# The sign step of a float64 to float32 conversion as a one-operand step on 16-bit halves, in a recurrent attention and MLP kernel

## The chip, the cores and the metric

One Trainium2 (trn2) chip; the program runs on one core. The metric is the device time of one execution in microseconds (us), as the median of several runs. Engines are named as in the profile: PE (TensorE), PEld (its weight loads), DVE (VectorE), ACT (ScalarE), POOL (GpSimd) and SP (SyncE, which issues most DMAs).

## The reference

```python
# attention: B=4, H=8, S=768, D=48, float32
state = zeros(B, H, D, D)
for t in range(S):
    cur = u * outer(k_t, v_t)
    y_t = r_t @ (state + cur)
    state = w * state + outer(k_t, v_t)
# then, with x = y as [4, 768, 384]:
h = x^T @ U @ V                  # U [768, 32], V [32, 768], over the sequence
u = x + h^T
ch = relu(u @ w_ch1) @ w_ch2     # w_ch1 [384, 1536], w_ch2 [1536, 384]
return (u + ch).astype(float32)
```

The four matrices U, V, w_ch1 and w_ch2 come in float64 (normal draws, scaled, that nothing casts down). The other inputs are float32.

## The kernel before, in words

The attention is computed in chunks of 128 positions, six for each of the four batch rows; each chunk has score matmuls (`pab`, L751), state updates (`pab`, L766) and outputs (`pav`, L787 and L793), with small DVE steps between them (`am` L885, `S` L913, `rT` L721, `x` L892). Then comes the MLP: for each half of a batch row (384 positions), twelve hidden blocks of 128 columns go through `m_1` (nine matmuls `p<-uTh,w1s` and `p<-uTl,w1s`) and `m_2` (nine matmuls `p<-w2s,hh` and `p<-w2s,hl`). Every operand is split into a high part, rounded to the matmul's format, and a low part, the rest; ACT makes the high parts (`uTh` L1012, `hh` L1080, `w1s` and `w2s` L548), DVE or POOL the low ones (`uTl` L1013, `hl` L1081, `w1s`/`w2s` L549). The MLP of one batch row runs while the attention of the next one is slipped in between its matmuls; the first row's attention has nothing beside it but the loads and the weights.

The weights are loaded as 64-bit words and made float32 on the chip, 27 units in all: `raw_u`, two `raw_v`, and 24 `raw_w` of 128x384 (twelve for w_ch1, twelve for w_ch2). `unit(...)` defines four steps for each, on the tile seen as pairs of 32-bit words, `word(0)` the lower and `word(1)` the upper:

- the byte step: the top byte of the lower word, scaled to 0..7, written over the lower word. These become the last three bits of the float32 mantissa. ACT (L522) or DVE (L518), by a choice of the planner.
- the scale step: the upper word, read as float32 and multiplied by 2^-112, which moves the exponent into place. ACT (L534).
- the sign step, `sign()`: the upper word's top bit is taken and joined to the lower word. DVE (L525).
- the join step, `join()`: the upper word shifted left by 3, joined to the lower word. DVE (L528).

Then the split follows: the cast on ACT (L548) and the difference on DVE or POOL (L549). All of this is done once, and most of it falls into the first MLP of the first batch row.

The order on each engine is written by the program itself. `Plan` holds every operation with a cost in ns and a key (its due place), simulates the engines, and emits the instructions in the order of its simulated starts; for an operation with several possible engines it picks one. Costs are formulas: `dve(n)` is 130 + 1.09 n for n elements per partition, `act(n)` is 285 + 0.6 n, a one-operand step on DVE is put at 100 + 0.65 n. `lock=True` marks operations that the planner keeps from running beside POOL's. The planner also puts in `wake` matmuls, whose result is not used, where it sees PE waiting before the MLP starts: once it waits longer than 150 ns. Each engine runs its own list in order, so what stands behind a waiting instruction waits too.

Of the kernel before, what the change touches and what calls it, by code (L numbers as in the profile page):

```python
# [14 lines left out]
U16 = mybir.dt.uint16  # L15
AF = mybir.ActivationFunctionType
ALU = mybir.AluOpType
# [29 lines left out]
class Plan:  # L47
# [28 lines left out]
    def op(self, eng, ns, fn, w=(), r=(), alt=(), lock=False, dma=0.0, rows=0, late=0.0, tiled=False, dk=0.0):  # L76


        if self.direct:
            fn()  # L80
            return None
        o = Op()
        o.n = len(self.ops)
        o.key = (self.key + dk, o.n)
        o.ways = [(eng, ns, fn, lock)] + list(alt)
        o.dma, o.rows, o.late, o.tiled = dma, rows, late, tiled
        o.deps, o.behind, o.allocs, o.bufs = set(), set(), [], []
        for acc, write in [(a, False) for a in r] + [(a, True) for a in w]:
            b, sub = acc if isinstance(acc, tuple) else (acc, None)
            if not b.uses and b.tag:  # L90
                o.allocs.append(b)
                ring = self.rings.setdefault(b.tag, {"order": [], "next": 0, "free": [(0.0, "")] * b.bufs, "last": None})
                ring["order"].append(b)
            elif b.tag and b.uses[0][0] is not o:
                o.behind.add(b.uses[0][0])
            for p, s, pw in b.uses:
                if (write or pw) and (s is None or sub is None or s == sub) and p is not o:
                    o.deps.add(p)
            b.uses.append((o, sub, write))
            if b not in o.bufs:  # L100
                o.bufs.append(b)
                b.left += 1
        self.ops.append(o)
        return o
# [171 lines left out]
def dve(n):  # L276
    return 130 + 1.09 * n


def act(n):  # L280
    return 285 + 0.6 * n
# [7 lines left out]
def rwkv_moe(ctx: ExitStack, tc: tile.TileContext, r, k, v, w, u, U, V, w1, w2, out):  # L289
    nc = tc.nc  # L290
# [30 lines left out]
    op = plan.op  # L321
# [30 lines left out]
    def on_act(n, fn, w_, r_, times=1, dk=0.0):  # L352
        return op("ACT", times * (act(n) - 94) + 94, fn, w_, r_, dk=dk)
# [10 lines left out]
    def dma(fn, w_, r_, rows, run, eng="SP", ns=470, dk=0.0, late=0.0, either=False):  # L364

        q = nc.scalar if eng == "ACT" else nc.sync
        return op(eng, ns, lambda: fn(q), w_, r_, dma=rows * max(1.08 if run < 500 else 0.96, run / 400),
                  rows=rows, late=late, dk=dk, alt=[("ACT", ns, lambda: fn(nc.scalar), False)] if either else ())
# [113 lines left out]
    def big(shape, dt, name):  # L482
        return xbuf(shape, dt, "big", NBIG, name)
# [3 lines left out]
    def unit(name, shape, parts, split):  # L487

        P_ = shape[0]
        n = 1  # L490
        for s_ in shape[1:]:
            n *= s_
        raw = big([128, 2 * n], I32, f"raw_{name}") if wide else big([128, n], F32, f"raw_{name}")

        def view(ap):
            return ap if len(shape) == 2 else ap.rearrange("p (a c) -> p a c", a=shape[1])

        loaded = [(raw, i) for i in range(len(parts))]

        def load():  # L500
            for i, (p0, ap) in enumerate(parts):
                dma(lambda q, p0=p0, ap=ap: q.dma_start(view(raw.t[p0:p0 + ap.shape[0]]), ap.bitcast(I32) if wide else ap),
                    [(raw, i)], [], ap.shape[0], (8 if wide else 4) * n, ns=370, late=LATE)

        def word(i):
            return raw.t[:P_].rearrange("p (n two) -> p two n", two=2)[:, i]

        def byte():
            return raw.t[:P_].bitcast(U8).rearrange("p (n e) -> p n e", e=8)[:, :, 3]

        def fl():
            return view(word(0).bitcast(F32) if wide else raw.t[:P_])

        def on_dve_byte():
            nc.vector.tensor_scalar(word(0), byte(), 2.0 ** -5, 7.0, ALU.mult, ALU.min)  # L518

        def on_act_byte():  # L520

            nc.scalar.activation(word(0), byte(), AF.Copy, scale=7.49 / 255)  # L522

        def sign():
            nc.vector.scalar_tensor_tensor(word(0), word(1), -2 ** 31, word(0), ALU.bitwise_and, ALU.bitwise_or)  # L525

        def join():
            nc.vector.scalar_tensor_tensor(word(0), word(1), 3, word(0), ALU.logical_shift_left, ALU.bitwise_or)  # L528

        def convert():  # L530
            if wide:
                op("DVE", 100 + 0.65 * n, on_dve_byte, [(raw, "lo")], loaded, lock=True,
                   alt=[("ACT", act(n) + 100, on_act_byte, False)])
                on_act(n, lambda: nc.scalar.activation(word(1).bitcast(F32), word(1).bitcast(F32), AF.Copy,  # L534
                                                       scale=2.0 ** -112), [(raw, "hi")], loaded)
                op("DVE", dve(n), sign, [(raw, "lo")], [(raw, "hi")], lock=True)
                op("DVE", dve(n), join, [(raw, "lo")], [(raw, "hi")], lock=True)
            split(fl, raw)
        return load, convert

    def weight_units():
# [14 lines left out]
        def v_split(j, sl):  # L556
# [4 lines left out]
            return go  # L561

        units.append(unit("u", [128, NCH, R], [(0, U.rearrange("(c p) r -> p c r", p=128))], u_split))
        for j in range(S // DM):
            sl = slice(j * DM, (j + 1) * DM)
            units.append(unit(f"v_{j}", [3 * R, DM], [(i * R, V[:, sl]) for i in range(3)], v_split(j, sl)))
        for g in range(FG):
            for ct in range(NCT):
                units.append(unit(f"w1_{ct}_{g}", [128, DM],
                                  [(0, w1[ct * 128:(ct + 1) * 128, g * DM:(g + 1) * DM])],  # L570
                                  split_to(W1, (ct, g), f"w1s_{ct}_{g}")))
            for f in range(g * NFT // FG, (g + 1) * NFT // FG):
                units.append(unit(f"w2_{f}", [128, DM], [(0, w2[f * 128:(f + 1) * 128, :])],
                                  split_to(W2, f, f"w2s_{f}")))
# [770 lines left out]
```

## Time and profile before

| | |
|---|---|
| time, median of 3 runs | 438.04 us (437.14 to 439.49) |
| the profiled execution | 439.95 us, of which the span from first to last instruction is 437.9 us |
| mean granted PE clock | 0.984 |
| busy | PE 96%, PEld 91%, DVE 61%, ACT 33%, POOL 13% |

The profile is of one execution, and its own time (439.95 us) is 1.91 us above the median. A matmul's row in the trace is longer than the distance to the next one, since matmuls overlap; what tells of lost time on PE is the idle time ahead of a group of matmuls and what released it. The span falls into the first attention with the weights' loads (0 to 56.2 us), the first MLP pieces with the rest of the conversion (56.2 to about 100 us), and matmuls back to back from there to 429 us.

### The profile page before, as it was taken

The page shows a single profiled execution, that of the slowest core. Times are in us where ns is not written, and L with a number is a line of the kernel's source. Part 1 is how long each engine was busy: PE and PEld are TensorE (multiplying, and loading weights), DVE is VectorE, ACT ScalarE, POOL GpSimd, SP SyncE. Part 2 cuts the span into 40 slices and gives each one's busy share as a digit, 9 for nine tenths or more (in the row PEclk, how much of TensorE's full clock was granted, in tenths as well). Part 3 has the DMA queues.
Part 4 walks back from the last instruction along what each step waited for, and adds up shares of the span by engine and source line. Part 5 has one row for each costly group of instructions (what it writes and reads, how often), then busy time and mean ns, then how long its engine had stood idle before and what let it go on. Part 6 is the DMA issues. An engine that isn't in the chain of part 4 may idle for free.

```text
span 437.9 us, 12193 instructions
## 1 busy us (share of the span) xinstructions
PE 419.4 (96%) x5125; PEld 399.8 (91%) x5125; DVE 267.8 (61%) x602; ACT 142.9 (33%) x399; POOL 55.6 (13%) x92
## 2 busy tenths in 40 slices
PE   8889999999999999999999999999999999999991
PEld 8678899889999999999999999999999999999991
DVE  6979699999887757767775456567522351122121
ACT  1679679934421213121112221222112131111110
POOL 2651151223110002011100001101100000000000
PEclk9989699999999999999999999999999999999998
DMA  9979999654466876744586653231100510001001
GB/s 145 162 162 340 335 199 222 103 84 83 81 88 139 148 146 117 136 87 76 105 168 102 96 147 56 48 64 30 55 2 1 98 65 1 0 0 55 1 0 61
DMA packets 178975, 43.93 MB, mean 100 GB/s; under 512 B 168993, under 2 KB 175650, under 8 KB 178914
## 3 DMA queue, kind: packets, MB, share of 16 engines
q1 hardware_dynamic: 174162, 42.20, 46.9%
q10 hardware_dynamic: 4752, 0.89, 1.5%
q8 instruction: 42, 0.69, 0.7%
q14 instruction: 19, 0.16, 0.1%
HBM read 36.57 MB, written 6.49 MB: 98 GB/s over the span
## 4 chain that ended last, share of the span: by engine, by line
PE 81%; DVE 8%; ACT 3%; DMA 3%; POOL 1%; issue 1%; SPq 0%; ACTq 0%; DVEq 0%; POOLq 0%
PE p L344 64%; PE pav L787 5%; PE pav L793 4%; PE pu L344 3%; DVE raw_w L528 2%; DVE raw_w L525 2%; PE pab L751 2%; DMA ld<-in_r_dram 1%; DMA ld<-in_v_dram 1%; PE pab L766 1%; PE wake L344 1%; DVE hl L1081 1%; PE pG L958 1%; ACT dv L681 1%; POOL dv L671 1%
## 5 line engine op out<-in xcount | busy, mean ns | idle before, releaser
L344 PE MATMUL p<-uTh,w1s 128*128 128x384 f32 x576 | 148.2, 338 | 0.0
L1081 DVE SCALAR_TENSOR_TENSOR hl<-p,hh 128x384 fp32r<-128x384 f32 x96 | 53.2, 554 | 119.3 <-ACT hh L1080 119.0
L344 PE MATMUL p<-w2s,hh 128*128 128x384 f32 x576 | 120.3, 340 | 0.6 <-ACT hh L1080 0.6
L1080 ACT ACTIVATE hh<-p 128x384 fp32r<-128x384 f32 x96 | 47.2, 491 | 210.3 <-PE p L344 208.7
L344 PEld LDWEIGHTS p<-uTh,w1s 128*128 128x128 f32 x576 | 102.9, 188 | 0.8
L344 PEld LDWEIGHTS p<-w2s,hh 128*128 128x128 f32 x576 | 99.8, 188 | 2.8 <-ACT hh L1080 0.9
L344 PE MATMUL p<-uTl,w1s 128*128 128x384 f32 x288 | 96.4, 335 | 0.0
L344 PE MATMUL p<-w2s,hl 128*128 128x384 f32 x288 | 65.8, 335 | 0.0
L344 PEld LDWEIGHTS p<-uTl,w1s 128*128 128x128 f32 x288 | 54.0, 188 | 0.0
L344 PEld LDWEIGHTS p<-w2s,hl 128*128 128x128 f32 x288 | 51.4, 188 | 0.0
L787 PE MATMUL pav<-vsw,am 64*64 64x48 f32 x384 | 33.0, 226 | 0.6 <-DVE am L885 0.5
L793 PE MATMUL pav<-S,rT 48*64 48x48 f32 x704 | 32.0, 222 | 0.9 <-issue 0.9
L787 PEld LDWEIGHTS pav<-vsw,am 64*64 64x64 f32 x384 | 26.7, 137 | 6.1 <-issue 4.1
L751 PE MATMUL pab<-rT,kT 48*64 48x64 f32 x768 | 31.2, 228 | 0.3 <-DVE rT L721 0.2
L793 PEld LDWEIGHTS pav<-S,rT 48*64 48x64 f32 x704 | 27.9, 139 | 1.0 <-issue 1.0
L751 PEld LDWEIGHTS pab<-rT,kT 48*64 48x64 f32 x768 | 25.1, 137 | 1.5 <-DVE rT L721 0.5
L787 PE MATMUL pav<-ldv,am 64*64 64x48 f32 x320 | 26.5, 222 | 0.0
L787 PEld LDWEIGHTS pav<-ldv,am 64*64 64x64 f32 x320 | 21.5, 134 | 4.7 <-issue 3.9
L885 DVE TENSOR_TENSOR am<-pab,mask 128x256 f32<-128x256 f32 x48 | 19.7, 417 | 6.8 <-PE pav L793 6.2
L661 POOL MEMSET ks<- 128x128 f32 x24 | 4.9, 205 | 133.2 <-PE pab L766 66.8
L766 PE MATMUL pab<-ldv,ks 64*48 64x48 f32 (+1 forms) x576 | 21.0, 212 | 0.0
L926 ACT ACTIVATE SW<-S,wm 112x48 f32<-112x48 f32 x48 | 12.2, 324 | 21.3 <-DVE S L913 20.0
(127 smaller groups left out, 515.5 us busy)
## 6 DMA issues: line engine op xcount, KB each, us to landing
raw_w<-in_moe_w_ch_dram SPq DMA_DIRECT2D x24, 384.0 KB, 7.4
out_dram<-x SPq DMA_DIRECT2D x24, 192.0 KB, 2.0
ldr<-in_r_dram SPq DMA_DIRECT2D x20, 192.0 KB, 3.3
ldk<-in_k_dram SPq DMA_DIRECT2D x20, 192.0 KB, 3.6
ldv<-in_v_dram SPq DMA_DIRECT2D x20, 192.0 KB, 3.6
bl<-in_r_dram SPq DMA_DIRECT2D x79, 48.0 KB, 2.6
bl<-in_k_dram SPq DMA_DIRECT2D x79, 48.0 KB, 2.5
vsw<-in_v_dram SPq DMA_DIRECT2D x42, 48.0 KB, 3.2
```

The costliest lines, as they stand in the source:

```text
L344: return nc.tensor.matmul(*args, **kw)
L525: nc.vector.scalar_tensor_tensor(word(0), word(1), -2 ** 31, word(0), ALU.bitwise_and, ALU.bitwise_or)
L528: nc.vector.scalar_tensor_tensor(word(0), word(1), 3, word(0), ALU.logical_shift_left, ALU.bitwise_or)
L661: op("POOL", 250, lambda: nc.gpsimd.memset(ks.t[:, :, D:], 0.0), [(ks, "pad")], [])
L751: return [lambda q=q, i=i: nc.tensor.matmul(pt.t[(i ^ j) * C2:(i ^ j) * C2 + C2, q * C2:(q + 1) * C2], lhsT=kT.t[rows, q, i * C2:(i + 1) * ...
L766: return nc.tensor.matmul(pt.t[j * HP:j * HP + m, SU + q * D:SU + (q + 1) * D], lhsT=ks.t[half, 2 * q + j, :m], rhs=vt()[half, 2 * q + j, ...
L787: return nc.tensor.matmul(to(q, j, i), lhsT=am[j].t[half, q, :], rhs=vsw[n].t[half, q, :] if j else vt()[half, 2 * q, :], start=(row == RO ...
L793: return nc.tensor.matmul(to(q, row, i), lhsT=rT.t[rows, q, i * C2:(i + 1) * C2], rhs=St[n, i].t[rows, q, :], start=False, stop=(row == RO ...
L885: on_dve(256, lambda e: e.tensor_tensor(am.t, abs_[n][j].t[:, :SU].rearrange("p (h t) -> p h t", h=NP), mask_.unsqueeze(1).broadcast_to([1 ...
L926: nc.scalar.activation(dec.t[:, q], new.t[:, q], AF.Copy, scale=wm.t[:, q])
L1080: on_act(384, lambda: nc.scalar.activation(hh.t, pt.t[:, :TB], AF.Relu), [hh], [pt])
L1081: on_dve(384, lambda e: e.scalar_tensor_tensor(hl.t, pt.t[:, :TB], 0.0, f32(hh.t), ALU.max, ALU.subtract), [hl], [pt, hh])
```

## The change

The sign step no longer has two operands. The byte step now writes its 0..7 as a 16-bit number into the lowest quarter of the 64-bit word (`half(0)`), instead of a 32-bit number over the lower word. The sign step takes the uppermost quarter (`half(3)`), keeps its top bit, and writes the result as a 16-bit number into the next quarter (`half(1)`), where the byte step's input stood. The two halves are then the lower word as it was before, and the join step is as it was. The planner's cost of the sign step goes from 130 + 1.09 n to 100 + 0.65 n, for n = 384 from 549 to 350 ns. Nothing else is edited; in the changed kernel line numbers behind this place are 3 higher.

```diff
+        def half(i):
+            return raw.t[:P_].bitcast(U16).rearrange("p (n e) -> p n e", e=4)[:, :, i]
+
         def on_dve_byte():
-            nc.vector.tensor_scalar(word(0), byte(), 2.0 ** -5, 7.0, ALU.mult, ALU.min)
+            nc.vector.tensor_scalar(half(0), byte(), 2.0 ** -5, 7.0, ALU.mult, ALU.min)

         def on_act_byte():
-            nc.scalar.activation(word(0), byte(), AF.Copy, scale=7.49 / 255)
+            nc.scalar.activation(half(0), byte(), AF.Copy, scale=7.49 / 255)

         def sign():
-            nc.vector.scalar_tensor_tensor(word(0), word(1), -2 ** 31, word(0), ALU.bitwise_and, ALU.bitwise_or)
+            nc.vector.tensor_scalar(half(1), half(3), 0x8000, None, ALU.bitwise_and)
...
-                op("DVE", dve(n), sign, [(raw, "lo")], [(raw, "hi")], lock=True)
+                op("DVE", 100 + 0.65 * n, sign, [(raw, "lo")], [(raw, "hi")], lock=True)
```

Since the planner's costs set the order, instructions move. In the rows below, `raw_w_1_1` and `raw_w_2_1` are units of w_ch1's second group, `w1s_1` their split parts, `raw_w_2` and `raw_w_3` units of w_ch2; the last number of a name is a running number of the build.

DVE before, from the last of the six `uTl` that open the MLP on:

```order
L1013 TENSOR_TENSOR uTl_1_1095<-pu_1_2_970,uTh_1_1086 128x384
L549 TENSOR_TENSOR w1s_1_1102<-raw_w_0_1_749,w1s_1_1102 128x384
L1081 SCALAR_TENSOR_TENSOR hl_0_0_1127<-p_0_0_0_1082,hh_0_0_1116 128x384
L528 SCALAR_TENSOR_TENSOR raw_w_1_1_787<-raw_w_1_1_787 128x384
L1081 SCALAR_TENSOR_TENSOR hl_0_1_1149<-p_0_0_1_1104,hh_0_1_1141 128x384
L525 SCALAR_TENSOR_TENSOR raw_w_2_1_792<-raw_w_2_1_792 128x384
L525 SCALAR_TENSOR_TENSOR raw_w_2_735<-raw_w_2_735 128x384
L528 SCALAR_TENSOR_TENSOR raw_w_2_1_792<-raw_w_2_1_792 128x384
```

DVE now, from the steps of the same two units to the first `uTl` (sign is L528 and join L531 in the new numbers):

```order
L528 TENSOR_SCALAR raw_w_1_1_787<-raw_w_1_1_787 128x384
L528 TENSOR_SCALAR raw_w_2_1_792<-raw_w_2_1_792 128x384
L531 SCALAR_TENSOR_TENSOR raw_w_1_1_787<-raw_w_1_1_787 128x384
L531 SCALAR_TENSOR_TENSOR raw_w_2_1_792<-raw_w_2_1_792 128x384
L951 TENSOR_TENSOR Gs_1052<-wake,Gs_1052 32x384
L552 TENSOR_TENSOR w1s_1_1063<-raw_w_0_1_749,w1s_1_1063 128x384
L552 TENSOR_TENSOR w1s_1_1070<-raw_w_1_1_787,w1s_1_1070 128x384
L1016 TENSOR_TENSOR uTl_0_1090<-pu_0_0_856,uTh_0_1080 128x384
```

The sign and join of both units stood behind the first MLP block's low part (`hl`) and now stand ahead of `uTl`; on ACT the three casts `w1s_1` stand ahead of the six `uTh` as well, where before they stood behind them.

PE before, at the end of the first attention, where `wake<-x,Uf` gathers x^T U and `pu<-V` multiplies it by V:

```order
L344 MATMUL pu_1_1_1024<-ident,x_968 128x128
L344 MATMUL pu_1_2_970<-ident,x_968 128x128
L344 MATMUL wake<-x_1029,Uf 96x128 x3
L344 MATMUL wake_1041<-ident 128x128
L344 MATMUL pu_1_0_1021<-ident,x_1029 128x128
L344 MATMUL pu_1_1_1024<-ident,x_1029 128x128
L344 MATMUL pu_1_2_970<-ident,x_1029 128x128
L344 MATMUL wake_1041<-ident 128x128 x2
L344 MATMUL pu_0_0_855<-V_817,Gs_1047 128x384
```

PE now, at the same place:

```order
L344 MATMUL pu_1_1_1028<-ident,x_972 128x128
L344 MATMUL wake<-x_1030,Uf 96x128 x3
L344 MATMUL wake_1042<-ident 128x128
L344 MATMUL pu_1_2_970<-ident,x_972 128x128
L344 MATMUL pu_1_0_1026<-ident,x_1030 128x128
L344 MATMUL pu_1_1_1028<-ident,x_1030 128x128
L344 MATMUL pu_1_2_970<-ident,x_1030 128x128
L344 MATMUL wake_1042<-ident 128x128 x3
L344 MATMUL pu_0_0_856<-V_810,Gs_1052 128x384
```

One `pu` goes behind the last gathering matmuls, and one unused matmul is added; a second one is added behind the six `pu<-V`, just ahead of the MLP's first matmul. Earlier in that attention a few `pu` change place by one or two matmuls. PE then keeps its order up to the third block's second layer. Before, in the first MLP piece (`p_0_0_3` is the fourth block's first layer, `w2s_1188` with `hh_0_2` the third block's second layer):

```order
L344 MATMUL p_0_0_3_1204<-uTh_0_1067,w1s_1_1102 128x384 x2
L344 MATMUL p_0_0_3_1204<-uTl_0_1076,w1s_1_1102 128x384
L344 MATMUL p_0_0_1130<-w2s_1188,hh_0_2_1194 128x384 x2
L344 MATMUL p_1_0_1133<-w2s_1188,hh_0_2_1194 128x384 x2
L344 MATMUL p_2_0_1135<-w2s_1188,hh_0_2_1194 128x384 x2
L344 MATMUL p_0_0_3_1204<-uTh_0_1067,w1s_1_1151 128x384 x2
```

And now:

```order
L344 MATMUL p_0_0_3_1224<-uTh_0_1080,w1s_1_1063 128x384 x2
L344 MATMUL p_0_0_3_1224<-uTl_0_1090,w1s_1_1063 128x384
L344 MATMUL p_0_0_3_1224<-uTh_0_1080,w1s_1_1070 128x384 x2
L344 MATMUL p_0_0_3_1224<-uTl_0_1090,w1s_1_1070 128x384
L344 MATMUL p_0_0_3_1224<-uTh_0_1080,w1s_1_1073 128x384 x2
L344 MATMUL p_0_0_3_1224<-uTl_0_1090,w1s_1_1073 128x384
L344 MATMUL p_0_0_1146<-w2s_1169,hh_0_2_1203 128x384 x2
```

The whole fourth first layer now comes ahead of `hh_0_2`'s use. Further on, where the second batch row's attention begins, three groups of PE move ahead of MLP matmuls: a transpose `ptr` ahead of one pair `p<-w2s,hh`, the first scores `pab` ahead of one `m_1` part of three matmuls, and the first outputs `pav` ahead of two pairs `p<-w2s,hh`. From the pair behind those on, PE's order is the same in both kernels to the end. DVE also takes over one byte step from ACT (`raw_w_0_0`) and two `kT` scalings of that attention.

## The prediction

> **What bounds the kernel now.** I read the slices first, for the stages; then PE's busy time stage by stage; then PE's waits; then the chain, for what stands behind the waits.
>
> ```profile
> PE   8889999999999999999999999999999999999991
> DVE  6979699999887757767775456567522351122121
> ...
> PEclk9989699999999999999999999999999999999998
> ```
>
> ```profile
> 56.20:65.90 9.70, 9.13 (x54) 8.79 (x52) 9.54 (x18) 8.13 (x21) 4.40 (x5) 1.00 0.93 179
> 65.90:100.00 34.10, 32.61 (x342) 30.51 (x343) 33.92 (x71) 26.38 (x73) 8.24 (x10) 1.00 0.71 135
> 100.00:150.00 50.00, 50.00 (x819) 46.47 (x819) 42.12 (x99) 14.13 (x50) 5.52 (x10) 1.00 0.59 109
> ...
> 200.00:300.00 100.00, 100.00 (x1263) 95.66 (x1262) 64.37 (x148) 22.70 (x63) 9.33 (x16) 1.00 0.53 97
> 300.00:429.10 129.10, 129.02 (x1051) 126.48 (x1049) 40.93 (x83) 22.77 (x49) 2.54 (x3) 1.00 0.09 24
> ```
>
> In each stretch the columns are its length and the busy time of PE, PEld, DVE, ACT, POOL. From 56.2 to 100 us two engines are full: DVE 9.54 of 9.70 and 33.92 of 34.10, PE all but 0.57 and 1.49 us. From 100 us on PE has no idle time worth the name, and DVE has plenty. So whatever DVE gains, the end can move only by PE's idle time ahead of 100 us, and by the time at which the MLP starts (56.2 us). PE's waits from 56 us to the end are these five, and no others:
>
> ```profile
> PE p L344 <- ACT hh L1080: 0.6, 1, 0.6
> PE pav L787 <- DVE am L885: 0.5, 1, 0.5
> PE ptr L712 <- ACT kT L727: 0.4, 1, 0.4
> PE pab L751 <- DVE rT L721: 0.2, 1, 0.2
> PE ptr L712 <- DVE kT L733: 0.2, 1, 0.2
> ```
>
> Together 1.9 us. The chain of work that ended last says otherwise at first sight: it gives DVE 8%, with the two conversion steps on it.
>
> ```profile
> PE 81%; DVE 8%; ACT 3%; DMA 3%; POOL 1%; issue 1%; SPq 0%; ACTq 0%; DVEq 0%; POOLq 0%
> ...
> 60.88 1.81 DVE raw_w L525 x2
> 62.69 1.30 DVE raw_w L528
> 64.06 0.43 ACT w1s L548
> ...
> 98.28 0.66 PE ptr L712 x4
> ```
>
> 8% of 437.9 us is 35 us, but it is the stretch from about 60 to 98 us, where DVE runs without a gap and PE beside it loses only those 1.9 us. The chain shows which engine was never waiting, not what its speed is worth.
>
> **The change part by part.** The sign step first: what it costs, and what a one-operand step costs.
>
> ```profile
> L525 DVE SCALAR_TENSOR_TENSOR raw_w<-raw_w x24: 544/548/1427, 40.0 to 96.0; 128x384 int32<-128x384 int32 x24
> L525 DVE SCALAR_TENSOR_TENSOR raw_w<-raw_w 128x384 int32<-128x384 int32 x17 | 10.3, 632 | 0.0
> L518 DVE TENSOR_SCALAR raw_w<-raw_w x1: 352/352/352, 39.8 to 39.8; 128x384 int32<-128x384 uint8 x1
> L470 DVE TENSOR_SCALAR wrc<-wrow 1x384 f32<-1x384 f32 x1 | 0.3, 341 | 0.0
> L892 DVE TENSOR_TENSOR x<-pav,dv 128x384 f32<-128x384 f32 x24 | 13.2, 549 | 1.4 <-PE pav L793 1.4
> ```
>
> A sign step takes 548 ns (median). Two rows show a one-operand step on 384 elements: 352 ns with one byte read and one word written in every 8 bytes, 341 ns on adjacent floats. The new step reads and writes 16 bits in every 8 bytes, which no row shows. It is nearest to the 352 ns row (same engine, same step of 8 bytes, a narrow operand on one side), so I take 352; the bounds are 341 below and, if two narrow operands cost the fast rate, the 548 of the two-operand form above. Each sign step then gives DVE 548 - 352 = 0.196 us. Seventeen of the 24 start between 56 and 100 us (second row): 17 x 0.196 = 3.3 us of DVE time there. The rest (seven `raw_w`, and `raw_u` and `raw_v`) lie ahead of 56 us.
>
> [...]
>
> The byte step's narrower output: on ACT the same bytes' row and the scale step's row are alike, so width has not mattered; I put it at 0, between -0.03 and +0.07 us a step (the spread of the first row around its median).
>
> ```profile
> L522 ACT ACTIVATE raw_w<-raw_w x23: 535/562/629, 39.0 to 84.0; 128x384 int32<-128x384 uint8 x23
> L534 ACT ACTIVATE raw_w<-raw_w x24: 535/568/627, 39.4 to 84.4; 128x384 f32<-128x384 f32 x24
> ```
>
> ACT is hidden behind DVE in that stage (26.4 of 34.1 us busy). One byte step moves from ACT to DVE: DVE +0.35 us at about 40 us, where two cheaper sign steps give it back (2 x 0.196).
>
> Now the waits. The 0.6 us wait for `hh` at 65.95 us goes back to ACT, which stood 1.57 us behind a `raw_w` join:
>
> ```profile
> 64.06 0.55 ACT L548 CAST w1s<-raw_w 128x384 fp32r<-128x384 f32 x1 [1.57 <-DVE raw_w L528]
> 65.95 1.55 PE L344 MATMUL p<-w2s,hh 128*128 128x384 f32 x6 [0.62 <-ACT hh L1080]
> ```
>
> In the new order that cast stands ahead of the MLP, and PE has six more matmuls ahead of the use of `hh_0_2`. I take it as gone: -0.62 us. The other four (0.5, 0.4, 0.2 and 0.2, together 1.3 us) all come in the second batch row's first chunk, 86 to 98 us, where DVE would by then be 3.3 us ahead. That would cover them several times over, but PE's order there was written for the faster DVE: `ptr` has moved up by a pair, `pab` by three matmuls, `pav` by two pairs, that is by up to 0.5, 0.8 and 1.0 us (1.55 us for six matmuls in the row above, 0.26 each). The planner packs until it sees no wait, and it was off by 0.2 to 0.5 us at these places before; I take half as staying: -0.65 us. Bounds: -1.3 and 0.
>
> The start of the MLP. First PE's last hole ahead of it and its busy time by the us (the granted clock is the last column but two), then the chain's `wake` pieces:
>
> ```profile
> 46.38 0.37 PE L793 MATMUL pav<-S,rT 48*64 48x48 f32 x5 [0.90 <-issue]
> ...
> 47.00:48.00 1.00, 1.00 (x22) 0.85 (x22) 0.42 (x1) 0.98 (x3) 0.00 (x0) 1.00 1.05 406
> 48.00:49.00 1.00, 1.00 (x23) 0.91 (x19) 0.14 (x1) 1.00 (x4) 0.00 (x0) 0.52 1.03 399
> ...
> 54.00:55.00 1.00, 1.00 (x8) 1.00 (x7) 1.00 (x1) 0.61 (x2) 1.00 (x2) 0.56 0.90 247
> 55.00:56.00 1.00, 1.00 (x8) 1.00 (x7) 0.33 (x2) 0.63 (x2) 1.00 (x1) 1.00 1.00 356
> ```
>
> ```profile
> 51.46 1.71 PE wake L344 x8
> ...
> 56.22 0.24 PE wake L344 x2
> ```
>
> PE runs full from about 47 us, and the new order has two more `wake` matmuls. One falls where eight take 1.71 us (0.21 each), one where two take 0.24 (0.12 each): +0.33 us if PE has no wait there for `Gs` and `uTh`, 0 if it has. Against it stands up to 0.2 us from one `pu` going behind the gathering matmuls. I take +0.2.
>
> Behind 100 us nothing is late next: PE has no wait to lose. What POOL does is moved by one or two splits. A sign step of one operand can still be held up beside POOL, as the 1427 ns in the first row was; that is in both kernels.
>
> Sum: -0.62 - 0.65 + 0.2 = -1.1 us. The profiled execution's own time is 439.95 us (span 437.9 and 2.05 around it), so a like execution of the changed kernel would take 438.9. That execution is 1.9 us above the median of the runs shown, 438.04; none of the three terms depends on it, so the median goes to about 436.9 us.
>
> **The rivals.** *PE's clock.* By the rows just shown PE runs at half clock just ahead of the MLP, from about 48 to 54.9 us, after a stretch with a hole of 0.90 us in it. If the moved matmuls shorten this by half, 3.4 us at half clock become 1.7: -1.7 us on top of the forecast, 435.2. If it grows by as much, 438.6. [...] The spread of the three runs (437.14 to 439.49) speaks for some of that in every run, not for a change by this edit. 0.17 for the gain.
>
> *Nothing comes of it.* PE's packed order turns the freed time into the same waits: the wait for `hh` goes, one like it comes elsewhere, the other four stay, and the two `wake` cost their 0.33: 438.4 us. For it: PE's order was packed to wait for nothing before as well, and waited 1.9 us. 0.18.
>
> *The step isn't faster* (slower than before). If the 16-bit form takes the 0.548 us of the old one, DVE is 17 x 0.196 = 3.3 us behind the order by 98 us, and PE, whose places were set for the faster step, stands behind `rT`, `am` and `hl`. If all of that is lost but the wait for `hh` goes all the same, the time is 438.04 + 0.2 + 3.3 - 0.62 = 440.9. It decides from the price at which 17 steps' lag eats the 1.1 us of the forecast: 0.352 + 1.1/17 = 0.42 us a step. Against it: both one-operand rows. 0.08.
>
> *Narrow words at a step cost more than one pass.* At twice the two-operand row, 1.10 us a step, DVE falls 17 x (1.10 - 0.352) = 12.7 us behind: 438.04 + 0.2 + 12.7 - 0.62 = 450.3. Against it: full rate at the same step of 8 bytes for words, and for the one byte operand. 0.02. [...]
>
> **How the numbers follow.** The forecast's own case has 0.53 (435.9 to 437.7, from -0.62 - 1.3 - 0.2 = -2.1 to -0.62 + 0.33 = -0.3 by the bounds of its terms), the clock 0.17, no effect 0.18, the step that isn't faster 0.08, the one that is slower 0.02, other things 0.02. About half a per cent, 2.19 us, is what a measurement here can tell from no change. The clock's gain and a small part of the forecast pass it: 0.25 for faster. Most of the two slow cases passes it, a longer cold stretch doesn't: 0.09 for slower. The remaining 0.66 is within. The range takes in the clock's 435.2 with a little for its spread, and, above, no effect with a cold stretch as much longer or a step half way to the slow one (438.04 + 1.4): 434.8 to 439.4.
>
> **What would show it.** Right: the sign row at about 350 ns in the changed profile; DVE with idle time between 75 and 100 us; no wait for `hh` near 66 us; PE's waits between 56 and 100 us down from 1.9 to about 0.65 us; PE's busy time behind 100 us unchanged. Wrong: a sign row of 450 ns or more; PE waits of over 2 us ahead of 100 us; a span that moved by more than 2 us while those waits did not, which would put the cause ahead of 56 us, in the clock column or in holes like the one at 45.5 us.

## The result, and the profile after

The changed kernel takes 444.78 us (median of 4 runs, 442.80 to 445.23); the kernel before took 438.76 us beside it (437.14 to 440.04). The ratio is 1.0143, with a 95% interval of 1.0108 to 1.0178: slower by 1.4%, where 436.9 us was forecast and 439.4 was the end of the range. The profiled execution took 445.23 us, with a span of 443.3 us; before it was 437.9, so the two traces are 5.4 us apart.

The answer to the rows of the prediction, first. These are the conversion steps of the w1 and w2 weights in the changed kernel (nanoseconds: shortest, median, longest; then first and last start):

```profile
L528 DVE TENSOR_SCALAR raw_w<-raw_w x24: 587/606/1541, 42.5 to 90.6; 128x384 uint16<-128x384 uint16 x24
L525 ACT ACTIVATE raw_w<-raw_w x22: 1034/1082/1159, 41.5 to 85.9; 128x384 uint16<-128x384 uint8 x22
L521 DVE TENSOR_SCALAR raw_w<-raw_w x2: 614/638/662, 40.4 to 40.7; 128x384 uint16<-128x384 uint8 x2
L531 DVE SCALAR_TENSOR_TENSOR raw_w<-raw_w x24: 534/553/808, 43.4 to 92.1; 128x384 int32<-128x384 int32 x24
```

The sign step (L528) takes 606 ns where it took 548: one operand fewer, and no gain. The byte step on ACT (L525) takes 1082 ns where it took 562, and on DVE (L521) 638 where it took 352. The join, which the change left alone, is what it was. The three steps that now write 16 bits are the three that became slower.

The same stretches as in the prediction, and four by 10 us (length; then busy time of PE, PEld, DVE, ACT and POOL; the granted clock follows):

```profile
56.20:65.90 9.70, 8.59 (x49) 8.05 (x49) 9.67 (x16) 9.69 (x20) 6.29 (x7) 1.00 1.05 265
65.90:100.00 34.10, 30.44 (x275) 28.97 (x274) 32.05 (x68) 26.08 (x53) 6.16 (x7) 0.95 0.57 97
50.00:60.00 10.00, 8.36 (x84) 7.66 (x85) 7.94 (x14) 9.93 (x21) 4.92 (x5) 1.00 1.01 265
60.00:70.00 10.00, 10.00 (x59) 9.79 (x58) 10.00 (x21) 9.99 (x20) 2.79 (x4) 1.00 0.80 213
70.00:80.00 10.00, 9.83 (x57) 9.51 (x56) 9.70 (x22) 10.00 (x22) 1.04 (x1) 1.00 0.65 102
80.00:90.00 10.00, 6.83 (x34) 6.39 (x33) 9.55 (x18) 8.76 (x17) 3.93 (x4) 0.83 0.36 58
```

ACT, the fourth busy column, has become a full engine from 50 to 80 us: 9.93, 9.99 and 10.00 of 10 us, where the trace of before has 6.70, 8.43 and 10.00. The total hides it: from 65.9 to 100 us ACT is as busy as before (26.08 against 26.38), because its work has moved forward and it ends sooner. PE pays: 4.77 us idle in the first two rows (1.11 and 3.66), where it had 2.06. The waits of PE from 57.4 us to the end:

```profile
PE ptr L715 <- DVE kT L736: 3.4, 2, 3.2
PE p L344 <- DVE uTl L1016: 1.1, 1, 1.1
PE pab L754 <- DVE rT L724: 0.3, 1, 0.3
PE p L344 <- ACT hh L1083: 0.2, 1, 0.2
```

5.0 us instead of 1.9. The wait for `hh` has indeed all but gone; the one for `kT` has grown to a hole. Here it is, on PE and then on DVE and ACT ahead of it:

```profile
82.30 0.34 PE L344 MATMUL p<-uTl,w1s 128*128 128x384 f32 x1
85.80 0.66 PE L715 MATMUL ptr<-ident,ldr 128*128 128x128 f32 x4 [3.17 <-DVE kT L736]
86.22 0.91 PE L344 MATMUL p<-Gs,V 96*128 96x384 f32 x3
86.92 2.12 PE L344 MATMUL p<-w2s,hh 128*128 128x384 f32 x6
```

```profile
80.98 0.56 DVE L552 TENSOR_TENSOR w2s<-raw_w,w2s 128x384 fp32r<-128x384 f32 x1 [0.20 <-ACT w2s L551]
...
82.32 0.60 DVE L528 TENSOR_SCALAR raw_w<-raw_w 128x384 uint16<-128x384 uint16 x1 [0.25 <-ACT raw_w L537]
82.71 0.58 DVE L531 SCALAR_TENSOR_TENSOR raw_w<-raw_w 128x384 int32<-128x384 int32 x1
83.22 0.54 DVE L1084 SCALAR_TENSOR_TENSOR hl<-p,hh 128x384 fp32r<-128x384 f32 x1
83.68 1.47 DVE L1123 TENSOR_TENSOR x<-p,x 128x384 f32<-128x384 f32 x3
85.07 0.68 DVE L736 TENSOR_TENSOR kT<-ptk,wi 112x512 f32<-112x512 f32 x1
```

```profile
80.79 1.15 ACT L525 ACTIVATE raw_w<-raw_w 128x384 uint16<-128x384 uint8 x1
81.61 0.68 ACT L537 ACTIVATE raw_w<-raw_w 128x384 f32<-128x384 f32 x1
82.12 0.53 ACT L1083 ACTIVATE hh<-p 128x384 fp32r<-128x384 f32 x1
```

`kT` stands on DVE in its written place, behind sign steps, joins, an `hl` and three `x`; the conversion steps wait for what ACT delivers (the brackets name ACT's cast and scale step), and ACT has no gap between its steps. In the kernel before, ACT made this `kT` (at 79.37 us); it is one of the two that the new order gave to DVE. So PE stands 3.17 us. The next six matmuls on `hh` take 2.12 us, where six took 1.31 at 78.79 us of the same trace: PE's clock has fallen to half.

```profile
86.00:87.00 1.00, 1.00 (x8) 1.00 (x8) 1.00 (x3) 1.00 (x3) 1.00 (x1) 0.85 0.00 0
87.00:88.00 1.00, 1.00 (x5) 1.00 (x4) 1.00 (x2) 1.00 (x4) 0.60 (x2) 0.50 0.25 42
88.00:89.00 1.00, 1.00 (x5) 1.00 (x4) 1.00 (x4) 0.20 (x1) 0.71 (x1) 0.50 1.15 215
89.00:90.00 1.00, 1.00 (x5) 0.91 (x4) 1.00 (x2) 0.55 (x1) 0.31 (x1) 0.50 0.68 96
90.00:91.00 1.00, 1.00 (x9) 1.00 (x8) 1.00 (x4) 0.30 (x1) 0.00 (x0) 0.94 0.70 104
```

In the clock column 0.15 + 3 x 0.50 + 0.06 = 1.71 us are lost, that is 3.4 us at half clock. With the MLP's first matmul at 57.48 us, which was at 56.20 before, the account is 1.3 (start) + 3.1 (waits) + 1.7 (clock) = 6.1 us, 0.7 more than the spans differ by; I can't say which term is counted twice. The start is also a matter of the clock: it was at half from 48.0 to 54.8 us in the trace of before and from 35.5 to 42.4 us in this one, and in the trace of the order alone (experiment 2), where it did not fall ahead of the MLP (mean clock 1.00 from 30 to 50 us), the MLP starts at 53.47 us. So the 1.3 us belong to these two executions, and not to the change alone.

### The profile page after: what moved, and what is told of

The parts are those of the page before. It is cut to its first block, busy times and chain, and to the rows that moved or that the text cites. A ratio compares the mean times of both kernels' runs of the same rounds, so it can differ in the third digit from the quotient of the medians.

```text
span 443.3 us, 12203 instructions
## 1 busy us (share of the span) xinstructions
PE 418.1 (94%) x5129; PEld 398.8 (90%) x5129; DVE 269.4 (61%) x607; ACT 148.7 (34%) x378; POOL 55.4 (12%) x92
## 4 chain that ended last, share of the span: by engine, by line
PE 80%; ACT 7%; SPq 4%; DVE 3%; DMA 3%; issue 1%; DVEq 0%; ACTq 0%
PE p L344 64%; PE pav L790 4%; PE pav L796 3%; SPq L621 3%; PE pu L344 2%; ACT raw_w L525 2%; PE pab L754 2%; DMA ub<-in_u_dram 1%; PE pab L769 1%; PE wake L344 1%; DMA raw_v<-in_moe_V_dram 1%; ACT raw_w L537 1%; DVE raw_w L528 1%; PE pG L961 1%; DMA wT<-in_w_dram 1%
## 5 line engine op out<-in xcount | busy, mean ns | idle before, releaser
L790 PE MATMUL pav<-vsw,am 64*64 64x48 f32 x384 | 32.1, 223 | 0.8 <-DVE am L888 0.7
L796 PE MATMUL pav<-S,rT 48*64 48x48 f32 x704 | 31.1, 219 | 1.1 <-issue 1.1
L754 PE MATMUL pab<-rT,kT 48*64 48x64 f32 x768 | 30.3, 224 | 0.3 <-DVE rT L724 0.3
L796 PEld LDWEIGHTS pav<-S,rT 48*64 48x64 f32 x704 | 26.9, 135 | 1.2 <-issue 1.2
L525 ACT ACTIVATE raw_w<-raw_w 128x384 uint16<-128x384 uint8 x22 | 24.0, 1090 | 0.0
```

What stands on the lines that cost most here:

```text
L525: nc.scalar.activation(half(0), byte(), AF.Copy, scale=7.49 / 255)
L754: return [lambda q=q, i=i: nc.tensor.matmul(pt.t[(i ^ j) * C2:(i ^ j) * C2 + C2, q * C2:(q + 1) * C2], lhsT=kT.t[rows, q, i * C2:(i + 1) * ...
L790: return nc.tensor.matmul(to(q, j, i), lhsT=am[j].t[half, q, :], rhs=vsw[n].t[half, q, :] if j else vt()[half, 2 * q, :], start=(row == RO ...
L796: return nc.tensor.matmul(to(q, row, i), lhsT=rT.t[rows, q, i * C2:(i + 1) * C2], rhs=St[n, i].t[rows, q, :], start=False, stop=(row == RO ...
```

## The experiments

What could be behind it? **Theory W**: a write of less than a word into every 8 bytes is slow, and ACT's byte step, 0.52 us longer, is nearly the whole loss. **Rival O**: the planner, told a sign step of 350 ns, wrote a bad order. **Rival S** (called L in a later run): not the order but the sign step's lag behind the price that the order was written for. Beside each run stands its ratio to the kernel before, measured on the same chip, with a 95% interval; it comes from all executions and need not be the quotient of the two medians.

**1. The prices by themselves.** Test steps behind the last matmul of the kernel before, each three times, on two idle scratch tiles; `vw` is every second word of a tile, `vh` every fourth 16 bits, `vb` every eighth byte:

```
+    for _ in range(3):
+        nc.vector.tensor_scalar(vh(sb, 1), vh(sa, 3), 0x8000, None, ALU.bitwise_and)
+    for _ in range(3):
+        nc.vector.tensor_scalar(vw(sb, 0), vh(sa, 3), 2.0 ** -5, 7.0, ALU.mult, ALU.min)
...
+    for _ in range(3):
+        nc.scalar.activation(vh(sb, 0), vb(sa, 3), AF.Copy, scale=0.5)
```

> The kernel before, with test steps behind its last matmul, on two scratch tiles, 384 elements a partition each, three of a kind, with nothing beside them (its time is longer by them and says nothing). Theory W (a write of less than a whole 4-byte word into every 8 bytes costs about twice, whatever is read): on DVE 16 bits to 16 bits about 600 ns, byte to 16 bits about 600, word to 16 bits about 600, byte to byte about 600, but 16 bits to word 350 and byte to word 350; on ACT byte to 16 bits about 1080, f32 to 16 bits about 1080, but 16 bits to word about 560; two adjacent 16-bit values in every 8 bytes, which fill a word, cost less than one alone. Rival R (16-bit or narrow reading at a step is what is slow): 16 bits to word about 600 on DVE and 1000 on ACT, word to 16 bits 350 and 560. Rival D (the 16-bit type, at any step): the adjacent 16-bit form is slow as well, about 600 on DVE. Rival C (contention: the steps are only slow beside the other engines' work): all of them 350 on DVE and 560 on ACT here.

The steps in this kernel's trace (L1333: 16 bits to 16 bits; L1337: 16 bits to word; L1339: word to 16 bits; L1341: byte to word; L1347: 16 bits at a step of 4 bytes; L1351: 16 bits at a step read, adjacent ones written; L1353: adjacent read, at a step written; L1359: two adjacent 16-bit values in every 8 bytes; on ACT L1363: byte to word, L1365: byte to 16 bits, L1367: byte to adjacent 16 bits, L1371: float word to 16 bits):

```profile
L1333 DVE TENSOR_SCALAR price_b<-price_a x3: 593/594/594, 432.7 to 433.9; 128x384 uint16<-128x384 uint16 x3
L1337 DVE TENSOR_SCALAR price_b<-price_a x3: 360/361/361, 436.4 to 437.2; 128x384 int32<-128x384 uint16 x3
L1339 DVE TENSOR_SCALAR price_b<-price_a x3: 593/593/594, 437.6 to 438.9; 128x384 uint16<-128x384 int32 x3
L1341 DVE TENSOR_SCALAR price_b<-price_a x3: 360/361/364, 439.5 to 440.3; 128x384 int32<-128x384 uint8 x3
L1347 DVE TENSOR_SCALAR price_b<-price_a x3: 424/427/428, 441.1 to 442.4; 128x384 uint16<-128x384 uint16 x3
L1351 DVE TENSOR_SCALAR price_b<-price_a x3: 359/360/360, 445.5 to 446.3; 128x384 uint16<-128x384 uint16 x3
L1353 DVE TENSOR_SCALAR price_b<-price_a x3: 578/582/594, 446.7 to 448.1; 128x384 uint16<-128x384 uint16 x3
L1359 DVE TENSOR_SCALAR price_b<-price_a x3: 260/261/263, 450.1 to 450.7; 128x384 uint16<-128x384 uint16 x3
L1363 ACT ACTIVATE price_b<-price_a x3: 539/539/539, 452.7 to 453.8; 128x384 int32<-128x384 uint8 x3
L1365 ACT ACTIVATE price_b<-price_a x3: 1051/1052/1052, 454.4 to 456.6; 128x384 uint16<-128x384 uint8 x3
L1367 ACT ACTIVATE price_b<-price_a x3: 540/541/541, 457.6 to 458.8; 128x384 uint16<-128x384 uint8 x3
L1371 ACT ACTIVATE price_b<-price_a x3: 1051/1052/1052, 462.6 to 464.8; 128x384 uint16<-128x384 f32 x3
```

Read them by the written side. Whatever is read, a lone narrow value written into every 8 bytes costs 582 to 594 ns on DVE (medians) and 1052 on ACT (1033 where 16 bits are read as well); a word written there costs 361 (394 in one form, a word read and its bits masked) and 539. Narrow values read at a step leave the step at 361 ns if a word is written (L1337) and at 360 if adjacent values are (L1351; 260 if they are also read adjacent), so it isn't reading; adjacent 16-bit values are cheap (L1359), so it isn't the type; no other engine had an instruction beside them, so it isn't contention. Theory W has its price.

**2. The change taken apart, in its own order.** Three kernels issue the same instructions in the same places on every engine as the changed one, apart from the form of one step or both:

```
 # sign only: the byte step, on ACT and on DVE, writes words again
-            nc.scalar.activation(half(0), byte(), AF.Copy, scale=7.49 / 255)
+            nc.scalar.activation(word(0), byte(), AF.Copy, scale=7.49 / 255)
 # order only: the same, and the sign step of two word operands
-            nc.vector.tensor_scalar(half(1), half(3), 0x8000, None, ALU.bitwise_and)
+            nc.vector.scalar_tensor_tensor(word(0), word(1), -2 ** 31, word(0), ALU.bitwise_and, ALU.bitwise_or)
 # byte only: the byte step as changed, and the sign step
+            nc.vector.scalar_tensor_tensor(word(0), word(1), -2 ** 31, word(1), ALU.bitwise_and, ALU.bitwise_and)
```

> The changed kernel, in its own order on every engine, but with the byte step writing the whole word again, on ACT and on DVE; the sign step keeps its 16-bit form. Theory W (the byte step's 16-bit write on ACT, 0.52 us a step, makes ACT the bound from 50 to 88 us and is nearly the whole loss): 438.5 to 441; the ACT byte row back at 0.56 us, ACT with idle time again in each 10 us from 50 to 90. Rival O (the planner, told a sign step of 350 ns, wrote an order with transposes and splits in bad places, and that order is the loss): 444 to 445.5. Rival S (the sign step of 0.61 us against 0.35 promised, 17 x 0.25 = 4.3 us behind by 98 us): 443 to 445.

> The changed kernel's order on every engine, but with both steps as they were before (the byte step writes a word, the sign step takes two words): nothing of the change but its order. Theory W: 438 to 440, the kernel before within half a per cent. Rival O: 444 to 445.5. Rival S: 442 to 444, since the order's places were set for 0.35 us a sign step and it has 0.55.

> The changed kernel in its own order, with the byte step's 16-bit write, but with a sign step of two word operands and a word written, as before; it overwrites the byte's bits (the lowest three bits of each weight's mantissa are left out). Theory W: 443.5 to 445.5, nearly the whole loss without the new sign step; the ACT byte row at about 1.08 us. Rival O: 444 to 445.5 as well (same order). Rival S: 443 to 444 by the order's lag alone, and no more with the slow ACT step than without it.

Sign only: 440.79 us, 1.0062 (1.0037 to 1.0086). Order only: 440.57 us, 1.0061 (1.0035 to 1.0087). Byte only: 444.78 us, 1.0150 (1.0118 to 1.0182). So the sign step's new form does nothing by itself; the byte step's 16-bit write costs 0.9%; and 0.6% comes from an order in which no step has changed. W alone, which gave the order 438 to 440 us, falls a little short here, and rival S, with 442 to 444, goes too far: the loss has two parts. PE's waits behind 53 us in the run with the order only:

```profile
PE ptr L715 <- DVE kT L736: 2.5, 2, 2.3
PE p L344 <- DVE uTl L1016: 0.5, 1, 0.5
```

The hole for `kT` is there already, 2.3 us long, with ACT's steps as fast as ever.

**3. Is the order bad, or late?** The same order with a sign step at the price that the planner was told; the same order with ACT's time spent without a narrow write; and both narrow steps in the old order:

```
 # cheap sign (the byte step writes words)
+            nc.vector.tensor_scalar(word(0), word(1), -2 ** 31, None, ALU.bitwise_and)
 # ACT twice
+            for _ in range(2):
+                nc.scalar.activation(word(0), byte(), AF.Copy, scale=7.49 / 255)
 # old order
-                op("DVE", 100 + 0.65 * n, sign, [(raw, "lo")], [(raw, "hi")], lock=True)
+                op("DVE", dve(n), sign, [(raw, "lo")], [(raw, "hi")], lock=True)
```

> The changed kernel's order, the byte step writing words, and a sign step of one word operand that writes a word (0.36 us in the price runs), so that the step has the price that the planner was told and the prediction took; it overwrites the byte's bits (the lowest three bits of each weight's mantissa are left out). Theory L (what the order alone cost, 0.6%, is lag: its places were set for 0.35 us a sign step and it got 0.55): the wait of PE's transposes for kT near 79 us goes, and the time is 436.5 to 438.5 (the prediction's own forecast, 436.9, where its price holds). Rival O (the order is bad whatever the step costs): 440 to 441.5, with that wait still there.

> The changed kernel's order with the byte step writing words, but on ACT executed twice in a row, 2 x 0.54 = 1.08 us of ACT time as in the changed kernel, with no 16-bit write by it (the second pass reads what the first wrote, so the byte's bits are left out). Theory W as occupancy (the 16-bit write only costs ACT its time): 444 to 446, the same loss as with one slow step; ACT full from 60 to 80 us. Rival C (the narrow writes disturb others as well, by way of the memory that they share): 441 to 443.5, clearly under the changed kernel.

> Both 16-bit steps in the order of the kernel before, on every engine (the planner is told the old cost of the sign step). If the two parts of the loss add up (the order 0.6%, ACT's byte step 0.9%): 441 to 443, 0.9% over before. If ACT's price is what counts and the order is only its first victim (theory W in its first form): 444 or more. Rival O (order alone): 437 to 439.

Cheap sign: 437.38 us, 0.9998 (0.9974 to 1.0021). Its sign row and what is left of the wait:

```profile
L528 DVE TENSOR_SCALAR raw_w<-raw_w x24: 345/354/1177, 40.5 to 82.0; 128x384 int32<-128x384 int32 x24
```

```profile
PE ptr L715 <- DVE kT L736: 1.0, 2, 0.8
PE pab L754 <- DVE rT L724: 0.5, 1, 0.5
```

At 354 ns a step the hole shrinks to 0.8 us and the 0.6% is gone: the order was late, not bad, and rival O falls. The run also tells what the change would have brought if its price had held: nothing that can be seen, though the forecast (436.9 on 438.04 us, 0.9974) lies at the very edge of the interval.

Old order: 443.87 us, 1.0132 (1.0106 to 1.0158), more than the 0.9% of adding parts, though that 0.9% is a difference of two ratios with intervals of their own, and the gap isn't clear of the noise. The planner's price of the sign step is off by little here (0.55 us told, 0.63 taken), and the cost is 1.3% all the same, most of it ACT's price: the parts seem to overlap. ACT made `kT` in this order, and PE waits 2.4 us for it there too. ACT twice: 448.06 us, 1.0239 (1.0212 to 1.0266). ACT's time alone, with ACT writing only words (the sign step on DVE still writes 16 bits), does all the harm and more, so nothing is left for a disturbance by ACT's narrow writes. That it does 3 us more than the changed kernel is explained in part: two passes take 2 x 562 ns against 1082, 22 x 0.042 = 0.9 us over the w1 and w2 steps, and behind its hole of 3.5 us PE's clock is at half for 6.8 us instead of 3.4, which is 1.7 us more.

**4. An order written for the true prices.** What is left is theory P: the order was set for false prices, the byte step's above all, and the engines' time as such would fit. The kernel with both 16-bit steps, where only what the planner is told differs: all prices as traced, or the sign step's alone, or the byte step's alone. And the first of these orders with the word-writing steps of before in it:

```
 # true costs ("true_again" is the same kernel); the next two have the last line alone, or the others alone
-                op("DVE", 100 + 0.65 * n, on_dve_byte, [(raw, "lo")], loaded, lock=True,
-                   alt=[("ACT", act(n) + 100, on_act_byte, False)])
+                op("DVE", 140 + 1.3 * n, on_dve_byte, [(raw, "lo")], loaded, lock=True,
+                   alt=[("ACT", 180 + 2.35 * n, on_act_byte, False)])
-                op("DVE", 100 + 0.65 * n, sign, [(raw, "lo")], [(raw, "hi")], lock=True)
+                op("DVE", 140 + 1.22 * n, sign, [(raw, "lo")], [(raw, "hi")], lock=True)
```

> Both 16-bit steps, with the planner told what the traces show: the sign step 0.61 us, the byte step 1.08 us on ACT and 0.64 us on DVE, so that it writes another order and moves two more byte steps to DVE. Theory W with lag: the order's part comes back, the price of ACT's step stays: 440 to 443. Rival O: with a fitting order everything comes back, 437 to 439. Rival B (the stage from 56 to 100 us is filled by DVE and ACT together, no order helps): 443.5 to 445.5.

> Both 16-bit steps; the planner is told the true 0.61 us for the sign step, and still the old prices for the byte step (0.62 us on ACT, 0.35 on DVE, where the traces have 1.08 and 0.64). Theory P (what costs is an order written for an ACT step of 0.62 us that takes 1.08; the sign step's price is the smaller lie): 442.5 to 444.5. Rival G (the sign step's price is what counts once it is told rightly): 436 to 439. Rival N (orders differ by luck, not by what the planner was told): anywhere from 436 to 445.

> Both 16-bit steps; the planner is told the true price of the byte step on both engines (1.08 and 0.64 us) and still 0.35 us for the sign step that takes 0.61. Theory P: most of the loss comes back, and what is left is the lag of the sign steps, as in the run with the order alone (0.6%): 437.5 to 440.5. Rival G: 443 to 445.

> The kernel with all prices told rightly once more, beside the next one on one chip: 435.5 to 437 by theory P; if its 0.4% under the kernel before was luck of that chip, 437 to 438.5.

> The order that was written for the true prices of the 16-bit steps, with the two steps of the kernel before in it, which write words and are cheaper by 0.52 us on ACT and 0.06 to 0.3 us on DVE. If the 16-bit steps still cost something in a fitting order: 434 to 436, faster than the last by 0.2% or more. If a fitting order hides all of it: the same as the last within 0.2%. If the gain over the kernel before belongs to the 16-bit steps: slower than the last, 437 to 438.5.

| planner told the true price of | us | ratio to before | interval |
|---|---|---|---|
| neither (the change) | 444.78 | 1.0143 | 1.0108 to 1.0178 |
| the sign step | 442.78 | 1.0105 | 1.0069 to 1.0141 |
| the byte step | 440.93 | 1.0053 | 1.0023 to 1.0084 |
| both | 436.06 | 0.9962 | 0.9937 to 0.9986 |
| both, on the chip of the next row | 436.20 | 0.9984 | 0.9949 to 1.0019 |
| both, with the word-writing steps put in | 436.04 | 0.9965 | 0.9938 to 0.9992 |

The rows of the sign step, of the byte step and the last two were measured on one chip, so their medians compare directly.

Of the kernel with true costs the theory that I then held, W with lag, expected 440 to 443, since ACT's price would stay; it came out under the kernel before, and under rival O's 437 to 439 as well. The byte step's false price counts for more (0.9% back when it is told rightly), the sign step's for less (0.4%, with intervals that overlap), as theory P had it, though 440.93 is a little above its 437.5 to 440.5; the rest comes only with both. Put into the fitting order, steps that are 0.52 us cheaper on ACT change nothing that shows (436.04 and 436.20): the order hides all of it. So the loss was not the steps' time as such, but their time in an order written for shorter steps. What the true prices changed shows from 56 to 100 us, first in the changed kernel, then with the true costs:

```profile
56.00:100.00 44.00, 39.23 (x322) 37.22 (x323) 41.72 (x83) 35.97 (x73) 12.65 (x14) 0.96 0.68 136
```

```profile
56.00:100.00 44.00, 43.49 (x468) 41.87 (x468) 43.40 (x90) 38.02 (x82) 16.80 (x20) 1.00 0.78 153
```

ACT does more in that stretch (38.02 us), DVE more (43.40), POOL 4.2 us more, and PE stands 0.5 us instead of 4.8. The planner has four byte steps on DVE instead of two, and this is the split (the difference step) that it put on POOL, with 8 of 24 in the changed kernel (two rows) and 15 with the true costs (two more):

```profile
L552 POOL TENSOR_TENSOR w1s<-raw_w,w1s x4: 1022/1024/1744, 44.6 to 88.3; 128x384 fp32r<-128x384 f32 x4
L552 POOL TENSOR_TENSOR w2s<-raw_w,w2s x4: 1017/1026/1037, 51.3 to 83.2; 128x384 fp32r<-128x384 f32 x4
```

```profile
L552 POOL TENSOR_TENSOR w1s<-raw_w,w1s x9: 1017/1041/1357, 44.1 to 88.8; 128x384 fp32r<-128x384 f32 x9
L552 POOL TENSOR_TENSOR w2s<-raw_w,w2s x6: 1023/1035/1102, 52.1 to 94.2; 128x384 fp32r<-128x384 f32 x6
```

So the true prices changed more than places: they moved work between engines as well. POOL's larger share alone isn't the cure, since the kernel with only the sign step's price told has 15 splits on POOL too and takes 442.78 us. How much of the rest is due to the places and how much to the choice of engines, no run separates. The remaining waits of PE behind 53 us with the true costs are 0.5 us (for `hl`) and 0.2 us (for `am`). Whether 0.2 to 0.4% under the kernel before is a gain of this order stays open: two of three intervals leave out 1, and all reach within half a per cent of it.

## Why the prediction was wrong

- **What bounds the stage.** Right as far as it went: PE's idle time ahead of 100 us and the start of the MLP moved, and PE's work behind 100 us is the same. A third thing moved that it had looked for only ahead of the MLP: PE's clock, with 1.7 us lost behind the hole for `kT`.
- **The sign step, 352 ns, bounds 341 and 548.** Wrong: 606 ns. The row that I called the nearest had its narrow operand on the read side, and the price runs show that narrow reading costs nothing where a word is written (361 ns with 16 bits, a byte or a word read); the written side decides. The upper bound was taken from a two-operand form that writes words, so it bounded nothing. The rival of narrow words that cost more than one pass had 1.10 us a step, an estimate, twice the row of 548 ns, and too high: the step takes 606 ns here and 594 in the price runs. What I held against it, that a step of 8 bytes costs words nothing (548 ns against 549 for the add on adjacent floats), was read from rows that write words; a word written there takes 361 ns in the price runs, and a lone narrow value 582 to 594. But that rival's direction, that the change might cost, was right, and I gave it 0.02.
- **The byte step's narrower output, put at 0 (-0.03 to +0.07 us).** This is the step that failed, with the sign step's price as the smaller part. I compared what is read, a byte in one row and a float in the other, and concluded that width does not matter; both rows write words. It costs 0.52 us on ACT, and of the loss 0.9%: 1.0150 in the run with the byte step alone against 1.0061 in the one with the order alone. The sign step's price gave the other 0.6%, as an order written for 0.35 us that got 0.55 or more.
- **"ACT is hidden behind DVE in that stage (26.4 of 34.1 us busy)".** True as a sum, and not a cover. From 56.2 to 100 us ACT had 1.57 + 7.72 = 9.3 us to spare, and 14 byte steps there now take 7.6 us more:

```profile
L522 ACT ACTIVATE raw_w<-raw_w 128x384 int32<-128x384 uint8 x14 | 7.9, 567 | 0.0
```

```profile
L525 ACT ACTIVATE raw_w<-raw_w 128x384 uint16<-128x384 uint8 x14 | 15.5, 1108 | 0.0
```

  It fits, as the kernel with true costs shows, which has 14 byte steps (15.3 us) on ACT in that stretch too; in an order that spaced ACT's steps for 0.62 us it doesn't, and DVE and then PE stand behind ACT.
- **The wait for `hh`, -0.62.** Right in the profile: the wait near 66 us is gone, and one of 0.2 us is left at 78.8 us. **The other four, -0.65:** wrong, the one for `kT` alone is 3.4 us. (The shifts that this term was weighed by used a row of 1.55 us for six matmuls; at 59.94 us of the same trace six take 1.24.) **The start of the MLP, +0.2:** it was +1.3, with the half-clock stretch at another place.
- **"Nothing comes of it", 438.4, 0.18.** With the step at my price, 0.9998: this was nearer to what the order could give than my forecast.
- **"The step isn't faster", 440.9, 0.08.** The lag was right, and the size came out: sign only measured 1.0062, which on 438.04 us is 440.8. The size was in part luck: the rival counted 3.3 us of waits, and with the order alone PE's waits grew by 1.1 us (3.0 against 1.9) and the clock lost 1.7, which the rival hadn't. It lacked the other step.
- **The range.** It reached half way to that rival, because the bounds of two unknown forms were narrow by the rows I took them from.

## What to carry to other kernels

Price a step by a row that matches on the side it writes, for every step of the change, also those that seem only to come along; where no row has that form, give it a factor of two upward (a lone narrow write took 593 ns against 361 on DVE, and 1052 against 539 on ACT). When a planner or a hand-written order sets places by costs, tell it the measured ones: here a kernel with the same steps took 444.8 us as planned by wrong prices and 436.1 as planned by right ones. An engine that is 80% busy in a stage covers added work only if the order leaves it room where the work falls.

## What the hardware showed that I had not expected

- A lone 16-bit or 8-bit value written into every 8 bytes: 582 to 594 ns against 361 to 394 for a word on DVE, 1033 to 1052 against 539 on ACT (384 elements, no other engine's work beside them); at a step of 4 bytes 427 on DVE. Two adjacent 16-bit values: 261. Why the writes are slow no run shows.
- Holes of 3.17 us (the changed kernel) and 2.31 us (its order alone) were each followed by 3.4 us at half clock: the clock column loses 1.71 us in both. How long a hole has to be, and why the stretch has this length, no run shows. In the kernel with only the byte step's prices told, PE's longest wait behind 50 us is 2.3 us, and the mean clock from 50 to 100 us is 0.97, as in the two above; in the one with only the sign step's it is 1.9 us, and the clock 1.00. For the order alone, these are the clock's rows:

```profile
79.00:80.00 1.00, 0.31 (x2) 0.31 (x3) 1.00 (x3) 1.00 (x4) 0.73 (x1) 0.80 0.23 34
80.00:81.00 1.00, 1.00 (x6) 1.00 (x5) 1.00 (x3) 0.78 (x2) 0.13 (x1) 0.50 0.00 0
...
83.00:84.00 1.00, 1.00 (x8) 0.97 (x7) 1.00 (x3) 0.41 (x1) 0.00 (x0) 0.99 0.79 116
```
